# Windowed attention and a SiLU MLP: three bits of each weight's low word by ScalarE's output conversion, and one VectorE instruction less per weight tile

## The chip, the cores and the metric

The kernel runs on one core of a Trainium2 chip. The metric is the device time of one execution in microseconds. Three executions of the kernel before took 979.6, 981.55 and 981.93 us; the median is 981.55 us.

## What is computed

```python
def _attn_ref(q, k, v):                       # q, k, v: (8, 8, 576, 64)
    scores = scale * np.matmul(q, k.transpose(0, 1, 3, 2))
    rel = pos[:, None] - pos[None, :]
    bias = slopes[:, None, None] * (-np.abs(rel).astype(np.float32))[None, :, :]
    mask = (rel >= 0) & (rel < 128)
    scores = np.where(mask, scores + bias[None], -1000000000.0)
    attn = np.exp(scores - np.max(scores, axis=-1, keepdims=True))
    attn = attn / (np.sum(attn, axis=-1, keepdims=True) + 1e-09)
    return np.matmul(attn, v).astype(np.float32)

x = attn_out.transpose(0, 2, 1, 3).reshape(4608, 512)
h = x @ w_in                                  # w_in: (512, 2048)
out = ((h / (1 + np.exp(-h))) @ w_out).astype(np.float32)   # w_out: (2048, 512)
```

q, k and v are float32. The two weight matrices are float64: each value arrives as two 32-bit words.

## The kernel before, in words

The 4,608 tokens are 36 tiles of 128; four tiles are one group of 512, so there are nine groups. Attention runs over pairs (a tile and half of its eight heads): `scores` (PE), `row_max` (VectorE, L311, adds the bias and takes the maximum out of PSUM), `exps` (ScalarE, L321), a split of the result in a high and a low 16-bit part (`p_hi` on ScalarE, L330, and `p_lo` on VectorE, L335), a transpose by DMA (`hl<-hr`), and `attend` (PE, `av`, L381). The MLP runs over 16 slices `f` of 128 hidden columns: `gemm1` makes `h` in two halves, `act1` to `act4` make `gt` and its high and low parts `gh` and `gl` (ScalarE L498 and L511, VectorE L503, GpSimd L118), `gemm2` adds to the outputs `o`, also in two halves.

Products of float32 accuracy are made from a high and a low part of each operand, so each weight tile is needed as two tiles. There are 32 weight tiles of 128 x 512 values, 16 of each matrix. A weight tile is loaded as 128 x 1024 words (`wr`, by `w_load`) and converted in five steps:

- `w_split1`, ScalarE, L581: reads the high words (every second word) as float32 and scales them into `wm`, so that sign and exponent come to stand where a float32 wants them after a shift;
- `w_shift`, VectorE, L587: shifts `wm` left by 3 bits, in place;
- `w_low`, VectorE, L592: shifts the low words (every second word of `wr`) right by 29 and joins the three bits to `wm` with an or;
- `w_hi`, ScalarE, L602: rounds `wm` to the high part `w`;
- `w_lo`, GpSimd, L118: subtracts the high part from `wm`, which gives the low part.

`wm` has two buffers (the pool's default, tag `io`), so a split waits for the subtraction of the weight tile two before it. The high and low parts of a tile take the place of its raw words.

The order on each engine is the order of the program. It walks through positions; a position is one half of a `gemm1` or `gemm2`. `put` and `later` enter steps in a plan by position, and `begin` issues those that are due. In the first group, whose slices come as `gemm1` half 0, half 1, `gemm2` half 0, half 1, `w_next` is called at each half 0: it issues the split of the next weight tile and enters the other steps at the positions given by `WD`, counted from the split (shift and join one later, high part two, low part three), and the load of the ninth tile ahead. Three tiles are begun before the first group. The scores of eight to ten pairs are spread over the first group by the table `CLOSE` and the function `at`; from this group on the scores and `av` share the two PSUM buffers of tag `a`, so that `attend` can begin only when VectorE has read the scores in front of it.

Of the kernel before, what the change touches and what calls it, by code (L numbers as in the profile page):

```python
# [8 lines left out]
F16 = mybir.dt.float16  # L9
BF16 = mybir.dt.bfloat16  # L10
I32 = mybir.dt.int32
AF = mybir.ActivationFunctionType
ALU = mybir.AluOpType
AX = mybir.AxisListType
# [31 lines left out]
SIGN_UP = -(2.0**32)  # L46


SLICE = 4


# [5 lines left out]
XD = GT  # L57
EARLY = ("w0_15", "w1_15", "w0_14", "w1_14", "w0_12", "w1_12", "w0_13")
AHEAD = 9
WD = (1, 1, 2, 3)  # L60

CLOSE = (1, 5, 8, 14, 20, 26, 32, 38)

# [1 line left out]
def at(p):  # L65

    if p < 2 * GT:
        return STEP * (p - 2 * GT) - 18
    if p < 4 * GT:
        return CLOSE[p - 2 * GT]  # L70
    return STEP * (p - 2 * GT) - LEAD
# [3 lines left out]
def tile_window_attention_then_silu_mlp(ctx, tc, qk, v, w_in, w_out, base8, out):  # L75
    nc = tc.nc
# [12 lines left out]
    wraw = {}  # L89
# [22 lines left out]
    def f32(ap):  # L112
        return ap.bitcast(F32)
# [41 lines left out]
    def vscale_reduce(b, i):  # L155
# [9 lines left out]
        else:  # L165
            junk = pool.tile([P, DM], F32, tag="gt", name=f"vj{b}_{i}") if b == 0 else t
            nc.scalar.activation(junk, t, AF.Abs, accum_out=m)

    wsc = {}

    def w_stat(which, f):

        if f == 0:
            vred["w", which] = {"m": pool.tile([P, NF], F32, tag=f"stat{which}", bufs=1, name=f"stat{which}")}
        junk = pool.tile([P, DM], BF16, tag="xs", bufs=2, name=f"wj{which}_{f}")
        nc.scalar.activation(
            junk, f32(w_parts(f, which)[0]), AF.Square, accum_out=vred["w", which]["m"][:, f : f + 1]
        )

    def vscale_finish(b, stage):  # L180
# [5 lines left out]
        elif stage == 1:  # L186
# [4 lines left out]
            nc.vector.tensor_reduce(c, ps[:1, :P], axis=AX.X, op=ALU.max)  # L191
            nc.vector.tensor_single_scalar(c.bitcast(I32), c.bitcast(I32), 0x7F800000, op=ALU.bitwise_and)
            if isinstance(b, tuple):
                ci = c.bitcast(I32)
                nc.vector.tensor_single_scalar(ci, ci, 1, op=ALU.logical_shift_right)
# [4 lines left out]
            inv = col[:1, 2:3]  # L200
            nc.vector.tensor_single_scalar(inv.bitcast(I32), c.bitcast(I32), -(14 << 23), op=ALU.add)
            nc.vector.tensor_scalar(c.bitcast(I32), c.bitcast(I32), -1, 268 << 23, op0=ALU.mult, op1=ALU.add)
        else:
# [113 lines left out]
    def exps(p, u):  # L317
        t, n = st[p]["t"][u], (2 - blocks(p).start) * P
        for h in range(2):
            x = t[:, h, 2 * P - n :]  # L320
            nc.scalar.activation(x, x, AF.Exp, bias=st[p]["mx"][:, 2 * u + h : 2 * u + h + 1], scale=-1.0)  # L321

    def split_of(p, u, what):
        n = 2 - blocks(p).start
        return what[:, : 4 * n * P].rearrange("p (a h c) -> p a h c", a=2, h=2)

    def p_hi(p, u):
        t, n = st[p]["t"][u], (2 - blocks(p).start) * P
        st[p]["hr", u] = hr = pool.tile([P, 8 * P], F16, tag="hr", bufs=2, name=f"hr{p}_{u}")
        nc.scalar.activation(split_of(p, u, hr)[:, 0], t[:, :, 2 * P - n :], AF.Copy, scale=PSCALE)  # L330

# [23 lines left out]
    def p_hi_first(p, u):  # L355
        n = 2 - blocks(p).start
        st[p]["hl"][u] = hl = pool.tile([P, 8, P], F16, tag="hl", bufs=4, name=f"hl{p}_{u}")
        hi = hl[:, : 2 * n].rearrange("p a c -> p (a c)")
        nc.scalar.activation(hi, st[p]["pt", u], AF.Copy, scale=PSCALE)

# [94 lines left out]
    def x_parts(i, part):  # L455
        t, first = xt[i & -2, "t"][:, i % 2], i % GT * P
        cols, scale = slice(first, first + P), vsc[i // NBLK][:, 1:2]
        if part == 0:
            nc.scalar.activation(xh[:, :, cols], t[:, :NCC], AF.Copy, scale=scale)
            return  # L460
# [106 lines left out]
    def w_load(f, which):  # L567
        t = pool.tile([P, 1024], I32, tag=f"w{which}_{f}", bufs=1, name=f"wr{f}_{which}")
        wraw[(f, which)] = t
        if which == 0:  # L570
            nc.sync.dma_start(
                t.rearrange("p (c f) -> p c f", c=NCC),
                w_in.bitcast(I32)[:, f * 2 * P : (f + 1) * 2 * P].rearrange("(c p) f -> p c f", p=P),
            )
        else:
            nc.sync.dma_start(t, w_out.bitcast(I32)[f * P : (f + 1) * P, :])

    def w_split1(f, which):
        t = wraw[(f, which)].rearrange("p (n w) -> p n w", w=2)
        m = pool.tile([P, DM], F32, tag="io", name=f"wm{f}_{which}")  # L580
        nc.scalar.activation(m, t[:, :, 1].bitcast(F32), AF.Prelu, scale=HI_SCALE, alpha=SIGN_UP)  # L581
        wraw[(f, which)] = (t, m)

    def w_shift(f, which):
        t, m = wraw[(f, which)]
        mi = m.bitcast(I32)
        nc.vector.tensor_single_scalar(mi, mi, 3, op=ALU.logical_shift_left)  # L587

    def w_low(f, which):
        t, m = wraw[(f, which)]  # L590
        mi = m.bitcast(I32)
        nc.vector.scalar_tensor_tensor(  # L592
            out=mi, in0=t[:, :, 0], scalar=29, in1=mi, op0=ALU.logical_shift_right, op1=ALU.bitwise_or
        )

    def w_parts(f, which):
        if which == 0:
            return [weight(kind, f).rearrange("p a b -> p (a b)") for kind in ("wih", "wil")]
        return weight("woh", f), weight("wol", f)
# [54 lines left out]
    def put(point, fn, *a):  # L654
        plan.setdefault(max(point, at(0)), []).append((fn, a))

    for p in range(NPAIR):
        i, q = divmod(p, 2)
        n = at(p)
        if p == 2 * GT - 1:  # L660
            a = n + 2 * STEP - 1
        elif p == 2 * GT:
            a = n + 10
        elif p == 2 * GT + 1:
            a = n + 12
        else:
            a = n + (2 * STEP + 2 if p < 2 * GT else 15 if p < 4 * GT else 13)
# [45 lines left out]
    for which, n in enumerate((CONV_IN, CONV_OUT)):  # L713
        for f in range(NF):
            for k, fn in enumerate((conv1, conv2, conv3)):
                put(n + SLICE * f + (k if which or f else 0), fn, which, f)
    for g in range(1, NG):
        put(at(2 * GT * g) + 10, x_unit, g)
        if g >= IN16:
            put(g * SLICE * NF - 2, mlp_scales, g)  # L720
    for b in range(1, NBB):

        n = at(2 * GT * (NBLK * b // GT)) + 2
# [8 lines left out]
    def later(n, fn, *a):  # L732
        put(pos[0] + n, fn, *a)
# [9 lines left out]
    def w_next():  # L743
        if wi[1] < len(wq):
            a = wq[wi[1]]
            wi[1] += 1
            w_split1(*a)
            for fn, n in zip((w_shift, w_low, w_hi, w_lo), WD):
                later(n, fn, *a)
            later(1, w_next_load)  # L750

# [4 lines left out]
    with tc.manual_schedule():  # L756
# [25 lines left out]
        for n in (-19, -7, -2):  # L782
            put(n, w_next)
# [7 lines left out]
        for g in range(NG):  # L791
# [3 lines left out]
            for f in range(NF):  # L795
                n = g * NF + f
# [3 lines left out]
            n = g * NF + NF - 1  # L800
            seq += [("g2", n - 1, 0), ("g2", n - 1, 1), ("g2", n, 0), ("g2", n, 1)]
            for k, n, half in seq:
                if k == "xt":
                    x_transpose(half)
                    continue
                begin()
                x_send()
                if k == "g1":
                    gemm1(n, half)
                    if half == 1:  # L810
                        act1(n)
                        if n % NF == NF - 1:
                            turn_over(n)
                        else:
                            later(1, act2, n)
                            later(2, act3, n)
                            later(2, act4, n)
                else:
                    gemm2(n, half)
                    if n % NF == NF - 1:  # L820
                        store(g, 2 * half)
                        store(g, 2 * half + 1)
                if g == 0 and half == 0:
                    w_next()
                pos[0] += 1
# [38 lines left out]
```

## Time and profile before

| | |
|---|---|
| median of three runs | 981.55 us |
| the profiled execution | 982.2 us |
| its span | 980.4 us |
| mean granted TensorE clock | 0.984 |
| busy: PE, VectorE, ScalarE, GpSimd | 942.7, 622.6, 481.2, 142.7 us |
| first and last start of a weight's split (L581) | 39.7 and 172.1 us |
| its chain that ended last: PE, VectorE, ScalarE | 81%, 10%, 3% |

In the profile, PE is TensorE's matmuls, PEld its weight loads, DVE VectorE, ACT ScalarE, POOL GpSimd and SP the engine that issues the transfers. A row of a group gives line, engine and operation, the tiles written and read with their shapes, the count, then the busy time, the mean length of one in ns, and the idle time of the engine ahead of it with what ended that. A row of a timeline begins with start and length in us from the start of the span. A chain is followed back from the last instruction, at each step to what released it.

### The profile page before, as it was taken

Reading aid. Unit: us, or ns where it says so; the run is one execution under the profiler, and the core shown is the slowest. Engines: PE = TensorE matmul, PEld = TensorE weight load, DVE = VectorE, ACT = ScalarE, POOL = GpSimd, SP = SyncE. Lnnn points to the kernel's source line nnn. Section 1 sums busy time; section 2 is a strip of 40 time slices with the busy share of each in tenths; the row PEclk is TensorE's granted clock in tenths of the full one; section 3 lists DMA queues with packets and bytes.
Section 4 is the critical chain, followed back from the end, with each engine's and each line's share of the span. In section 5 each row is a group of like instructions: output and inputs, shape, how many; then the busy total and the mean of one; then the engine's idle time right before and its main releaser. Section 6 shows DMA issues by size and latency. Waiting matters only on the chain.

```text
span 980.4 us, 17282 instructions
## 1 busy us (share of the span) xinstructions
PE 942.7 (96%) x6572; PEld 581.6 (59%) x6572; DVE 622.6 (64%) x1567; ACT 481.2 (49%) x984; POOL 142.7 (15%) x129
## 2 busy tenths in 40 slices
PE   7978988999998999999999999999999999999998
PEld 6856766777776887654545554554555545554443
DVE  4888999655676887876666665555655565553222
ACT  5665665667553554555444445444544454433222
POOL 3154555222211222100000000000000000000000
PEclk8998999999998999999999999999999999999999
DMA  7848982423334543432364535332434343321001
GB/s 248 300 118 217 242 215 49 119 65 86 78 69 124 119 119 79 116 87 66 88 149 119 119 97 130 87 87 65 130 86 88 86 129 87 65 55 54 1 1 43
DMA packets 201075, 104.95 MB, mean 107 GB/s; under 512 B 168224, under 2 KB 176416, under 8 KB 200992
## 3 DMA queue, kind: packets, MB, share of 16 engines
q1 hardware_dynamic: 200992, 103.84, 41.4%
q8 instruction: 52, 0.85, 0.4%
q14 instruction: 31, 0.25, 0.1%
HBM read 54.00 MB, written 9.44 MB: 65 GB/s over the span
## 4 chain that ended last, share of the span: by engine, by line
PE 81%; DVE 10%; ACT 3%; DMA 2%; issue 2%; SPq 0%; POOL 0%; ACTq 0%; DVEq 0%; POOLq 0%
PE o L551 32%; PE h L485 30%; PE sp L291 7%; PE h L490 6%; PE av L381 5%; DVE wm L587 2%; DVE wm L592 2%; DMA early<-v 1%; DVE v L273 1%; DVE t L311 1%; DVE hr L335 1%; DVE gt L503 1%; ACT wm L581 1%; DMA hl<-hr 1%; ACT gt L498 1%
## 5 line engine op out<-in xcount | busy, mean ns | idle before, releaser
L551 PE MATMUL o<-w,gh 128*128 128x512 f16 (+1 forms) x1152 | 354.2, 389 | 0.0
L485 PE MATMUL h<-xt,w 128*128 128x512 f16 (+1 forms) x1536 | 317.8, 354 | 0.0
L498 ACT ACTIVATE gt<-h,gsc 128x512 f32<-128x512 f32 x112 | 77.1, 688 | 319.2 <-PE h L485 317.2
L551 PE MATMUL o<-w,gl 128*128 128x512 f16 (+1 forms) x576 | 222.8, 387 | 1.2 <-POOL gl L118 1.2
L485 PEld LDWEIGHTS <-w 128*128 128x128 f16 x1536 | 143.7, 98 | 130.8 <-issue 2.4
L503 DVE SCALAR_TENSOR_TENSOR gt<-gt,h 128x512 f32<-128x512 f32 x144 | 98.7, 686 | 176.6 <-ACT gt L498 176.3
L551 PEld LDWEIGHTS <-gh 128*128 128x128 f16 x768 | 74.9, 98 | 88.6
L321 ACT ACTIVATE t<-t,mx 128x256 f32<-128x256 f32 (+1 forms) x288 | 121.5, 486 | 12.0 <-DVE mx L311 11.9
L311 DVE CUSTOM_DVE_ANT_0 t<-sp,tab 128x256 f32<-128x256 f32 (+1 forms) x288 | 102.3, 403 | 18.6 <-PE sp L291 11.9
L519 DVE SCALAR_TENSOR_TENSOR gl<-gt,gh 128x512 f16<-128x512 f32 x96 | 66.5, 693 | 74.8 <-ACT gh L513 74.7
L335 DVE SCALAR_TENSOR_TENSOR hr<-t,hr 128x512 f16<-128x512 f32 (+1 forms) x128 | 99.2, 793 | 23.3 <-ACT hr L330 23.3
L490 PE MATMUL h<-xh,w 128*128 128x512 f32 x256 | 92.6, 416 | 4.6 <-ACT xh L434 3.6
L262 POOL TENSOR_SCALAR v<-rv,vsc 128x512 f16<-128x512 f32 x32 | 25.1, 785 | 444.4 <-DMA rv<-v 335.2
L118 POOL TENSOR_TENSOR gl<-gt,gh 128x512 fp32r<-128x512 f32 x45 | 63.2, 1405 | 177.5 <-ACT gh L511 141.5
L291 PEld LDWEIGHTS sp<-k,q 64*128 64x128 f32 x1088 | 69.5, 192 | 32.1 <-issue 31.1
L291 PE MATMUL sp<-k,q 64*128 64x128 f32 x1088 | 83.9, 291 | 4.7 <-DVE xs L408 4.6
L513 ACT ACTIVATE gh<-gt 128x512 f16<-128x512 f32 x96 | 60.0, 624 | 47.5 <-DVE gt L503 47.2
L551 PEld LDWEIGHTS o<-w,gh 128*128 128x128 f32 x384 | 71.9, 193 | 16.3 <-ACT gh L511 0.3
L381 PE MATMUL av<-v,hl 128*128 128x65 f16 (+1 forms) x1632 | 63.1, 194 | 15.3 <-DVE mx L311 8.4
L330 ACT ACTIVATE hr<-t 128x512 f16<-128x512 f32 (+1 forms) x128 | 75.9, 598 | 3.6 <-DMA hl<-hr 3.6
L381 PEld LDWEIGHTS <-hl 128*128 128x128 f16 x1632 | 58.5, 98 | 31.8 <-issue 19.0
L551 PEld LDWEIGHTS <-gl 128*128 128x128 f16 x384 | 37.5, 98 | 47.8 <-DVE gl L519 3.5
(99 smaller groups left out, 789.2 us busy)
## 6 DMA issues: line engine op xcount, KB each, us to landing
q<-qk SPq DMA_DIRECT2D x36, 256.0 KB, 3.0
k<-qk SPq DMA_DIRECT2D x36, 256.0 KB, 3.1
out<-ot SPq DMA_DIRECT2D x36, 256.0 KB, 2.4
wr<-w_in SPq DMA_DIRECT2D x16, 512.0 KB, 6.8
wr<-w_out SPq DMA_DIRECT2D x16, 512.0 KB, 6.0
rv<-v SPq DMA_DIRECT2D x32, 256.0 KB, 2.9
vm<-v SPq DMA_DIRECT2D x27, 256.0 KB, 3.3
early<-v SPq DMA_DIRECT2D x9, 256.0 KB, 5.2
```

Of the source, the lines that this page charges most:

```text
L291: nc.tensor.matmul(sp[h][:, u, o], qs[i][rows, 2 * q + u], ks[i - 1 + o][rows, 2 * q + u], start=True, stop=True, skip_group_check=True,)
L311: nc.vector.tensor_tensor_reduce(out=t[:, h, 2 * P - n :], in0=st[p]["sp"][h][:, u, o].rearrange("p o c -> p (o c)"), in1=tab[:, 4 * q + 2 ...
L321: nc.scalar.activation(x, x, AF.Exp, bias=st[p]["mx"][:, 2 * u + h : 2 * u + h + 1], scale=-1.0)
L330: nc.scalar.activation(split_of(p, u, hr)[:, 0], t[:, :, 2 * P - n :], AF.Copy, scale=PSCALE)
L335: nc.vector.scalar_tensor_tensor(out=hr[:, 1], in0=t[:, :, 2 * P - n :], scalar=PSCALE, in1=hr[:, 0], op0=ALU.mult, op1=ALU.subtract)
L381: nc.tensor.matmul(av[:, 2 * u + h, : rhs.shape[-1]], lhs, rhs, start=(n == 0), stop=(n == len(seq) - 1), skip_group_check=True,)
L485: nc.tensor.matmul(o, w[:, wp, cc], x, start=start and k == 0, stop=stop, skip_group_check=True)
L490: nc.tensor.matmul(hps[n], w[:, cc], x, start=(half == 0 and i == 0), stop=(half == 1 and i == len(seq) - 1), skip_group_check=True,)
L498: nc.scalar.activation(gt, hps[n], AF.Tanh, scale=scale)
L503: nc.vector.scalar_tensor_tensor(out=gt, in0=gt, scalar=1.0, in1=hps[n], op0=ALU.add, op1=ALU.mult)
L519: nc.vector.scalar_tensor_tensor(out=gl, in0=gt, scalar=CUT, in1=gh, op0=ALU.mult, op1=ALU.subtract)
L551: nc.tensor.matmul(ops[ti], a[:, t], w, start=(f == 0 and i == 0), stop=(f == NF - 1 and i == len(seq) - 1), skip_group_check=True,)
```

## The change

ScalarE gets a second conversion for each weight tile, directly behind the split: it reads the low words as unsigned integers, scales them by nearly 2^-29 and adds a bias, so that the conversion of its output to an integer leaves the top three bits as a number from 0 to 7; this is written back in place of the low word. VectorE's two instructions become one, which shifts `wm` left by 3 and joins the number with an or. The separate shift is gone, and `WD` has one entry less; the other steps keep their positions.

```diff
+LOW3 = 2.0**-29 * (1 - 2.0**-10)
+LOW3_UP = 7.5 * 2.0**-10 - 0.5
...
-WD = (1, 1, 2, 3)
+WD = (1, 2, 3)
...
-    def w_shift(f, which):
-        t, m = wraw[(f, which)]
-        mi = m.bitcast(I32)
-        nc.vector.tensor_single_scalar(mi, mi, 3, op=ALU.logical_shift_left)
-
-    def w_low(f, which):
+    def w_low3(f, which):
+
+        t, _ = wraw[(f, which)]
+        low = t[:, :, 0]
+        nc.scalar.activation(low, low.bitcast(U32), AF.Copy, scale=LOW3, bias=LOW3_UP)
+
+    def w_join(f, which):
         t, m = wraw[(f, which)]
         mi = m.bitcast(I32)
         nc.vector.scalar_tensor_tensor(
-            out=mi, in0=t[:, :, 0], scalar=29, in1=mi, op0=ALU.logical_shift_right, op1=ALU.bitwise_or
+            out=mi, in0=mi, scalar=3, in1=t[:, :, 0], op0=ALU.logical_shift_left, op1=ALU.bitwise_or
         )
...
             w_split1(*a)
-            for fn, n in zip((w_shift, w_low, w_hi, w_lo), WD):
+            w_low3(*a)
+            for fn, n in zip((w_join, w_hi, w_lo), WD):
                 later(n, fn, *a)
```

The order of the instructions changes on VectorE and ScalarE alone. One place in the first group, first VectorE's queue of the kernel before, from the join of one weight tile (`wm_0_1447`) to the first row maximum of the second half of a pair (`t_1_1515`); ISA is the row maximum and its read-out:

```order
L592 SCALAR_TENSOR_TENSOR wm_0_1447<-wr_0_1006,wm_0_1447 128x512
L120 SCALAR_TENSOR_TENSOR x_1469<-xs_1449,x_1469 128x256
L311 ISA t_0_1494,mx_1482<-sp_0_1472,tab 128x256
L311 ISA mx_1482 128x1
L311 ISA t_0_1494,mx_1482<-sp_1_1473,tab 128x256
L311 ISA mx_1482 128x1
L164 TENSOR_REDUCE vmx_884<-vm_5_1415 128x1
L587 TENSOR_SCALAR wm_1_1492<-wm_1_1492 128x512
L592 SCALAR_TENSOR_TENSOR wm_1_1492<-wr_1_1063,wm_1_1492 128x512
L311 ISA t_1_1515,mx_1482<-sp_0_1472,tab 128x256
```

And the same place after the change (its lines are four or five further down; L597 is the new join):

```order
L597 SCALAR_TENSOR_TENSOR wm_0_1447<-wm_0_1447,wr_0_1006 128x512
L124 SCALAR_TENSOR_TENSOR x_1469<-xs_1450,x_1469 128x256
L315 ISA t_0_1495,mx_1482<-sp_0_1472,tab 128x256
L315 ISA mx_1482 128x1
L315 ISA t_0_1495,mx_1482<-sp_1_1473,tab 128x256
L315 ISA mx_1482 128x1
L168 TENSOR_REDUCE vmx_884<-vm_5_1416 128x1
L597 SCALAR_TENSOR_TENSOR wm_1_1492<-wm_1_1492,wr_1_1063 128x512
L315 ISA t_1_1515,mx_1482<-sp_0_1472,tab 128x256
```

One instruction in front of the row maxima is gone, and nothing else has moved. ScalarE's queue at this place before, from the high part of that weight tile to the exponentials (L321) of the pair's second half:

```order
L602 CAST w_8_1483<-wm_0_1447 128x512
L581 ACTIVATE wm_1_1492<-wr_1_1063 128x512
L498 ACTIVATE gt_1513<-h_1485 128x512
L321 ACTIVATE t_0_1494<-t_0_1494,mx_1482 128x256 x2
L602 CAST w_7_1522<-wm_1_1492 128x512
L581 ACTIVATE wm_0_1531<-wr_0_1122 128x512
L321 ACTIVATE t_1_1515<-t_1_1515,mx_1482 128x256 x2
```

And after the change (L592 is now the new conversion on ScalarE):

```order
L607 CAST w_8_1483<-wm_0_1447 128x512
L585 ACTIVATE wm_1_1492<-wr_1_1063 128x512
L592 ACTIVATE wr_1_1063<-wr_1_1063 128x512
L502 ACTIVATE gt_1513<-h_1485 128x512
L325 ACTIVATE t_0_1495<-t_0_1495,mx_1482 128x256 x2
L607 CAST w_7_1522<-wm_1_1492 128x512
L585 ACTIVATE wm_0_1531<-wr_0_1122 128x512
L592 ACTIVATE wr_0_1122<-wr_0_1122 128x512
L325 ACTIVATE t_1_1515<-t_1_1515,mx_1482 128x256 x2
```

Behind each split there is one more instruction, ahead of the hidden activation and of the exponentials. The transfers, GpSimd's and PE's queues are as before.

More of the change, by code (lines that the diff above doesn't have):

```diff
@@ L11 @@
 I32 = mybir.dt.int32
+U32 = mybir.dt.uint32
 AF = mybir.ActivationFunctionType
```

## Prediction

> **What bounds the kernel now.** I read the head of the page first, then the windows by stage, because a share of the whole span mixes stages.
>
> ```profile
> span 980.4 us, 17282 instructions
> PE 942.7 (96%) x6572; PEld 581.6 (59%) x6572; DVE 622.6 (64%) x1567; ACT 481.2 (49%) x984; POOL 142.7 (15%) x129
> ```
>
> PE is busy for 96% of the span, so only the places where PE is idle or slow can give anything back. The weights are converted while the first group of tokens is multiplied. The tile of the converted word, `wm`, tells when that is:
>
> ```profile
> L581 ACT ACTIVATE wm<-wr x32: 657/668/692, 39.7 to 172.1; 128x512 f32<-128x512 f32 x32
> L587 DVE TENSOR_SCALAR wm<-wm x32: 404/981/1521, 40.4 to 172.8; 128x512 int32<-128x512 int32 x32
> L592 DVE SCALAR_TENSOR_TENSOR wm<-wr,wm x32: 691/693/1679, 40.8 to 173.8; 128x512 int32<-128x512 int32 x32
> ```
>
> All of it starts between 39.7 and 173.8 us. The windows (length, then busy us of PE, PEld, DVE, ACT and POOL, then the granted clock, the DMA share and GB/s) of the two halves of this stage and of three short stretches:
>
> ```profile
> 62.00:134.60 72.60, 63.85 (x417) 49.61 (x416) 66.69 (x137) 46.35 (x92) 39.10 (x28) 0.93 0.89 222
> 134.60:178.00 43.40, 40.00 (x264) 31.57 (x264) 39.09 (x74) 25.52 (x50) 26.10 (x20) 1.00 0.42 109
> 76.90:80.30 3.40, 3.40 (x10) 2.63 (x10) 2.96 (x7) 1.24 (x3) 0.00 (x0) 0.56 1.49 239
> 90.50:93.90 3.40, 3.40 (x30) 2.82 (x27) 3.33 (x7) 3.40 (x9) 2.14 (x2) 0.57 0.78 292
> 128.10:131.50 3.40, 3.40 (x30) 2.83 (x28) 2.62 (x7) 1.96 (x5) 1.28 (x1) 0.56 1.21 223
> ```
>
> While weights are converted, VectorE is busy 66.69 of 72.60 us (92%) and then 39.09 of 43.40 (90%). ScalarE is busy only 64% and 59%. PE is idle 8.75 + 3.40 = 12.15 us, and in three stretches of 3.4 us its clock is 0.56, so each costs it about 1.5 us more. Who keeps PE waiting, in the list of waits of 40 to 184 us (total, times, longest):
>
> ```profile
> PE av L381 <- DVE mx L311: 8.4, 7, 2.4
> PE h L490 <- ACT xh L434: 3.6, 1, 3.6
> PE av L381 <- DMA q<-qk: 2.2, 1, 2.2
> PE sp L291 <- DVE xs L408: 1.1, 1, 1.1
> ```
>
> The attention products `av` wait for VectorE's row maxima (L311), which release the PSUM buffer that `av` takes. Those instructions are late because VectorE reaches them late. The chain that ended last, cut to 36 to 178 us, says what made it late:
>
> ```profile
> by line: DVE wm L587 14.9%; DVE wm L592 13.6%; PE h L490 10.1%; issue 9.8%; DVE hr L335 7.0%; ACT wm L581 5.4%; DMA hl<-hr 4.7%; DVE v L273 3.6%; DVE t L311 3.4%; DVE gt L503 3.1%; PE o L551 2.9%; DMA vm<-v 2.1%; DVE vmx L164 2.0%; PE av L3
> ```
>
> Of these 142 us the shift (L587) holds 21.2 and the join (L592) 19.3. So a microsecond saved there is, to begin with, a microsecond of the program.
>
> **The change: what VectorE is spared.** 32 shifts go; they take 27.1 us in all, by the row of the group:
>
> ```profile
> L587 DVE TENSOR_SCALAR wm<-wm 128x512 int32<-128x512 int32 x32 | 27.1, 848 | 5.5 <-ACT wm L581 5.2
> ```
>
> But a shift alone takes 0.40 us (its shortest, above) against a mean of 0.85; the rest is waiting inside the instruction. The next rows show for what, and the place that I re-lay by hand. It is the timeline of 106 to 118 us, first VectorE's, then ScalarE's and GpSimd's (start, length):
>
> ```profile
> 109.12 1.52 DVE L587 TENSOR_SCALAR wm<-wm 128x512 int32<-128x512 int32 x1
> 110.67 0.69 DVE L592 SCALAR_TENSOR_TENSOR wm<-wr,wm 128x512 int32<-128x512 int32 x1
> ...
> 112.90 0.83 DVE L587 TENSOR_SCALAR wm<-wm 128x512 int32<-128x512 int32 x1
> 113.77 0.69 DVE L592 SCALAR_TENSOR_TENSOR wm<-wr,wm 128x512 int32<-128x512 int32 x1
> ...
> 115.80 1.02 DVE L587 TENSOR_SCALAR wm<-wm 128x512 int32<-128x512 int32 x1
> 116.85 0.69 DVE L592 SCALAR_TENSOR_TENSOR wm<-wr,wm 128x512 int32<-128x512 int32 x1
> ...
> 111.45 0.62 ACT L602 CAST w<-wm 128x512 fp32r<-128x512 f32 x1 [2.79 <-DVE wm L592]
> 111.98 0.67 ACT L581 ACTIVATE wm<-wr 128x512 f32<-128x512 f32 x1
> 112.55 0.58 ACT L498 ACTIVATE gt<-h 128x512 f32<-128x512 f32 x1
> 113.03 0.89 ACT L321 ACTIVATE t<-t,mx 128x256 f32<-128x256 f32 x2
> 114.55 0.62 ACT L602 CAST w<-wm 128x512 fp32r<-128x512 f32 x1 [0.62 <-DVE wm L592]
> ...
> 108.60 1.75 POOL L118 TENSOR_TENSOR gl<-gt,gh 128x512 fp32r<-128x512 f32 x1
> 112.15 1.30 POOL L118 TENSOR_TENSOR w<-wm,w 128x512 fp32r<-128x512 f32 x1 [1.80 <-ACT w L602]
> 115.24 1.28 POOL L118 TENSOR_TENSOR w<-wm,w 128x512 fp32r<-128x512 f32 x1 [1.80 <-ACT w L602]
> ```
>
> GpSimd's subtraction ends at 110.35, 113.45 and 116.52, and each long shift ends 0.3 us behind that: it got to work 0.1 us before GpSimd was done. So shift and join can be held by a GpSimd instruction (the join's longest is 1.68 us). The join usually escaped (median 0.693) because the shift ahead of it had sat out the wait. By the medians the join would cost 0.69 and VectorE would be spared all 27.1 us. [...] So I count 32 x 0.40 = 12.9 us of VectorE time as gone and the 14.2 us of waiting as mostly inherited.
>
> **What ScalarE gets.** 32 more conversions. No row shows this one (unsigned integer in, integer out, every second word written). The nearest row is L581, which reads every second word of the same tile and takes 0.67; below it lies L602 with 0.62 (above), and as the upper end I allow two passes, 1.34. I take 0.67. In ScalarE's queue it costs 0.57, the distance from L581 to L498 (111.98 to 112.55). That is 18 us more in a stage in which it is idle for over a third; but ScalarE works in order, so the exponentials, `gt` and `gh` behind each split come 0.57 later than the split lets them, and the join has to wait for the second conversion.
>
> **Re-laid by hand**, with the first join ready at 109.12: it is held till 110.24, ends at 110.93 and not at 111.36 (0.43 gained). ScalarE's L602 follows at 111.02, L581 at 111.55, the new conversion from 112.12 to 112.79; GpSimd has the port till about 112.90. VectorE is ready at 112.47, so the second join runs from 112.90 to 113.59 instead of ending at 114.46: 0.87 gained, and the `av` that waits for the two row maxima behind it comes 0.87 earlier. For the third weight ScalarE is the one behind: L498 and the exponentials end at about 114.06, so L602 starts at 113.97 (0.58 earlier), the new conversion ends at 115.74, GpSimd's port is free at 115.85, the join ends at 116.54, not 117.54. The exponentials behind it start at 115.64 instead of 115.66, so what waits for them on VectorE gains only about 0.6. Three weights thus give between 0.6 and 1.0: 0.2 to 0.33 each, and 0.43 where nothing behind it is late. Where VectorE waits for the split anyway, the loop of one weight is this:
>
> ```profile
> 137.74 0.67 ACT L581 ACTIVATE wm<-wr 128x512 f32<-128x512 f32 x1
> ...
> 138.44 1.05 DVE L587 TENSOR_SCALAR wm<-wm 128x512 int32<-128x512 int32 x1 [0.29 <-ACT wm L581]
> 139.53 0.69 DVE L592 SCALAR_TENSOR_TENSOR wm<-wr,wm 128x512 int32<-128x512 int32 x1
> ...
> 137.91 1.29 POOL L118 TENSOR_TENSOR w<-wm,w 128x512 fp32r<-128x512 f32 x1 [1.33 <-ACT w L602]
> ```
>
> Now it ends at 140.22. After the change the conversion ends at 137.74 + 0.57 + 0.67 = 138.98, GpSimd at 139.20, and the join at 139.89: 0.33 gained.
>
> **The sum.** 21.2 us of shifts on the path at 0.85 are 25 weights; at 0.3 each that is 7.5 us (0.2 gives 5.0; 0.43 gives 10.8). The three slow-clock stretches follow the longest waits of PE, 2.2 to 2.4 us; waits of about 1.1 us are followed by none there. With 0.9 off, some go: 3 x 1.5 us, of which I take half, since VectorE still bounds the stage: 2.2 (0 to 4.5). At the start PE waits 3.6 us for ScalarE's `xh` (L434), which has two splits in front of it; there the conversion comes on top, less the shift's wait between them: 0.6 lost (0 to 1.2). 7.5 + 2.2 - 0.6 = 9.1; the ends are 3.8 and 15.3. The stages behind contain no weight conversion and stay. The profiled execution took 982.2 us, 1.8 around its span, and 0.65 over the median of 981.55; so 973.1 on its own scale and **972.5** against the median.
>
> **Rivals.**
>
> *More: PE is fed.* If VectorE's spared time also breaks up the meetings with GpSimd (joins pass before GpSimd starts), PE's 12.15 us of idle time and the 4.5 us of slow clock go almost whole: 14 to 16.6, about 966. For it: with all 27 us gone, VectorE's 105.8 busy us of these 116 (91%) would be about 79 (68%). Against it: GpSimd's subtraction follows L602, and the join follows the next split, so they keep meeting.
>
> *Nothing: the path goes over ScalarE.* In the hand-laid piece the third weight was already ScalarE's. If the exponentials, `hr` and `gh` are late by 0.57 in most rounds, or the `hl` transfers (4.7% of the chain, under a DMA share of 0.89) decide, the 7.5 shrink to under 3 and the slow stretches stay: about 980.
>
> *Less: the strided write is dearer.* No ScalarE row writes every second word. If the new conversion takes 1.0 us, midway between 0.67 and 1.34, the loop at 137 us gains nothing (138.98 becomes 139.31, and the join ends at 140.0 to 140.2), the second weight of the hand-laid piece gains 0.6 and the third about 0.3. At 0.2 for the 25 weights and no slow stretch less, 5 - 0.6 = 4.4 are left: about 977.5. L581's strided read, 0.05 over L602, speaks against it. [...]
>
> *Slower: the new conversion takes two passes.* It turns the sign from about 1.1 us on. At 1.34, the loop loses 0.34 for each of the 12 splits on the chain (5.4% of 142 us at 0.67), 4 us; the exponentials behind the others come over 1 us late, which eats what their joins gain: about 986. For it speaks only that no row converts to an integer on ScalarE; against it, that L581 and L602 differ in function, type and stride and lie within 0.05.
>
> That the join is not what it says (two inputs swapped, a shift in front of an or) I price at nothing: the same form already runs in 0.69 with its strided input.
>
> **Chances.** The forecast 0.65, more 0.12, nothing 0.12, less 0.04, slower 0.07. About 0.3% (3 us) is what a measurement of this kernel can tell from no change. The forecast's lower end, 3.8, is still outside that, and so is "less": faster 0.81, same 0.12, slower 0.07. The range takes in the forecast's two ends and a little of both neighbours: 966 to 979.
>
> **What would show it.** Right: `wm` has one VectorE row with a mean well over 0.69 (0.9 to 1.1, waits inherited), the new ScalarE row at 0.62 to 0.72, VectorE still busy for 85 to 90% of the stage, the waits of `av` for L311 at about half of 8.4 us, one or two slow-clock stretches fewer, and everything behind the first group shifted and otherwise alike. Wrong: a ScalarE row over 1 us; waits of VectorE for `hr` (L335) or `gt` that grow by what the shift gave; or a join at 0.69 in the mean, which would mean that the wait for GpSimd went with the shift.

## The result, and the profile after

The changed kernel's median is 971.95 us over four runs (970.19 to 974.15), beside 980.85 us for the kernel before; the ratio on record is 0.9901, with a 95% interval of 0.9872 to 0.993 (the two medians alone give 0.9909). Measured once more later, beside other kernels, it gave 971.93 us and 0.9904 (0.988 to 0.9928). It is faster by about 9 us; the prediction was 972.5 us, faster by 9.1. One run of the kernel before among the later ones, 1197.39 us at a granted clock of 0.75, is left out of every comparison.

The head of the page after:

```profile
span 971.5 us, 17272 instructions
PE 938.7 (97%) x6572; PEld 578.0 (59%) x6572; DVE 597.0 (61%) x1535; ACT 497.3 (51%) x1016; POOL 141.6 (15%) x129
```

VectorE has lost 25.6 us of busy time and ScalarE gained 16.1, and the span is 8.9 us shorter. The conversion of the weights, by the instructions on `wm` (L597 is the new join, L607 the high part) and by those on the raw words `wr` (L592 is the new conversion):

```profile
L585 ACT ACTIVATE wm<-wr x32: 649/665/689, 40.5 to 163.3; 128x512 f32<-128x512 f32 x32
L597 DVE SCALAR_TENSOR_TENSOR wm<-wm,wr x32: 679/716/1777, 41.7 to 164.6; 128x512 int32<-128x512 int32 x32
L607 ACT CAST w<-wm x32: 603/618/624, 42.5 to 165.4; 128x512 fp32r<-128x512 f32 x32
```

```profile
L592 ACT ACTIVATE wr<-wr x32: 647/658/672, 41.0 to 163.9; 128x512 int32<-128x512 uint32 x32
```

The first split starts 0.8 us later than before (40.5, was 39.7), the last 8.8 us earlier (163.3, was 172.1). The 0.8 us are no cost of the change: they stand ahead of the first new instruction, and the first splits of the fourteen profiles lie between 39.3 and 41.0 us. The groups add the idle time ahead of the join, which the shift and the old join had as 5.5 and 1.1 us. First the old join before, then the new join after:

```profile
L592 DVE SCALAR_TENSOR_TENSOR wm<-wr,wm 128x512 int32<-128x512 int32 x32 | 27.0, 845 | 1.1
```

```profile
L597 DVE SCALAR_TENSOR_TENSOR wm<-wm,wr 128x512 int32<-128x512 int32 x32 | 29.4, 918 | 15.0 <-issue 8.0 <-ACT wr L592 7.0
```

The scores, one instruction group per pair, show where on the way the time was won. Their starts before (start, length), at five places of the first group and the next:

```profile
62.10 1.16 PE L291 MATMUL sp<-k,q 64*128 64x128 f32 x16
...
82.55 1.16 PE L291 MATMUL sp<-k,q 64*128 64x128 f32 x16
...
134.59 1.16 PE L291 MATMUL sp<-k,q 64*128 64x128 f32 x16
...
172.29 1.16 PE L291 MATMUL sp<-k,q 64*128 64x128 f32 x16
...
189.23 0.72 PE L291 MATMUL sp<-k,q 64*128 64x128 f32 x8
```

and after:

```profile
62.60 1.16 PE L295 MATMUL sp<-k,q 64*128 64x128 f32 x16
...
78.74 1.34 PE L295 MATMUL sp<-k,q 64*128 64x128 f32 x16
...
129.13 1.16 PE L295 MATMUL sp<-k,q 64*128 64x128 f32 x16
...
163.83 1.16 PE L295 MATMUL sp<-k,q 64*128 64x128 f32 x16
...
179.21 0.72 PE L295 MATMUL sp<-k,q 64*128 64x128 f32 x8
```

0.5 us behind at 62 us, 3.8 ahead two pairs later, 5.5 at 134, 8.5 at 172, 10.0 at 189; from there to the start of the last product (976.19 us before, 966.43 after) the distance stays within 0.3, and behind it 0.9 us are lost on the way to the spans' 8.9. Of the 10.0, 8.5 are won while weights are converted; up to 3 of these are two slow-clock stretches fewer between 62 and 178 us, three before and one after, at an estimated 1.5 us each (3.4 us at a clock of 0.56 to 0.58). The last 1.5 come behind the last split: the profile before has a slow-clock stretch there, which the profile after lacks:

```profile
182.70:186.10 3.40, 3.35 (x26) 2.87 (x26) 1.80 (x3) 1.47 (x3) 0.00 (x0) 0.56 0.62 45
```

The windows of the stage after the change, with the one slow-clock stretch that is left between 62 and 178 us, and PE's waits:

```profile
62.00:134.60 72.60, 66.93 (x454) 51.60 (x454) 58.30 (x133) 58.74 (x116) 41.56 (x30) 0.98 0.97 238
134.60:178.00 43.40, 40.94 (x278) 32.36 (x278) 32.37 (x74) 33.52 (x65) 22.45 (x17) 1.00 0.35 89
121.90:125.30 3.40, 2.72 (x28) 2.46 (x29) 1.90 (x9) 3.06 (x6) 1.28 (x1) 0.58 0.98 213
```

```profile
PE av L385 <- DVE mx L315: 5.5, 5, 2.4
PE h L494 <- ACT xh L438: 3.2, 1, 3.2
PE av L385 <- DVE v L277: 1.7, 2, 1.2
```

PE's idle time in the first window fell from 8.75 to 5.67 us, its clock rose from 0.93 to 0.98, and VectorE is busy 80% instead of 92%. In the chain, cut to 36 to 170 us, VectorE's work on `wm` held 28.5% before:

```profile
by line: PE h L494 15.7%; PE o L555 10.4%; DMA vm<-v 10.0%; issue 8.5%; DMA hl<-hr 5.2%; DVE wm L597 4.9%; DMA wr<-w_out 4.6%; PE sp L295 4.4%; ACT wr L592 3.2%; DVE v L277 3.0%; ACT t L325 3.0%; ACT wm L585 2.9%; PE av L385 2.6%; ACT hr L3
```

Now the join has 4.9% of it, the new conversion 3.2%. PE's products lead, and the transfers `vm<-v`, `hl<-hr` and `wr<-w_out` hold 19.8% together.

### The profile page after: what moved, and what is told of

Its sections match the earlier page's. It is cut to its first block, busy times and chain, and to the rows that moved or that the text cites. A ratio compares the mean times of both kernels' runs of the same rounds, so it can differ in the third digit from the quotient of the medians.

```text
span 971.5 us, 17272 instructions
## 1 busy us (share of the span) xinstructions
PE 938.7 (97%) x6572; PEld 578.0 (59%) x6572; DVE 597.0 (61%) x1535; ACT 497.3 (51%) x1016; POOL 141.6 (15%) x129
## 4 chain that ended last, share of the span: by engine, by line
PE 84%; DVE 5%; DMA 4%; ACT 4%; issue 2%; SPq 1%; POOL 0%; ACTq 0%; DVEq 0%; POOLq 0%
PE o L555 33%; PE h L489 30%; PE sp L295 7%; PE h L494 7%; PE av L385 5%; DMA vm<-v 1%; DMA early<-v 1%; DVE v L277 1%; DVE t L315 1%; DMA hl<-hr 1%; DVE gt L507 1%; DVE wm L597 1%; DMA wr<-w_out 1%; ACT gt L502 1%; PE pt L357 1%
## 5 line engine op out<-in xcount | busy, mean ns | idle before, releaser
L339 DVE SCALAR_TENSOR_TENSOR hr<-t,hr 128x512 f16<-128x512 f32 (+1 forms) x128 | 93.4, 747 | 24.4 <-ACT hr L334 24.4
L122 POOL TENSOR_TENSOR gl<-gt,gh 128x512 fp32r<-128x512 f32 x45 | 60.1, 1336 | 185.2 <-ACT gh L515 142.8
L555 PEld LDWEIGHTS o<-w,gh 128*128 128x128 f32 x384 | 69.9, 188 | 16.5 <-ACT gh L515 1.2
```

Source lines behind the costliest of these rows:

```text
L339: nc.vector.scalar_tensor_tensor(out=hr[:, 1], in0=t[:, :, 2 * P - n :], scalar=PSCALE, in1=hr[:, 0], op0=ALU.mult, op1=ALU.subtract)
L555: nc.tensor.matmul(ops[ti], a[:, t], w, start=(f == 0 and i == 0), stop=(f == NF - 1 and i == len(seq) - 1), skip_group_check=True,)
```

## The experiments

The theory: VectorE's queue sets the time of the stage; the bare instruction is gone, the wait for GpSimd is inherited, the conversion is nearly hidden. The rivals: ScalarE carries the path now, or VectorE's waits are slack. Ratios are to the kernel before, on the same chip, with 95% intervals. For each kernel the row of its VectorE instructions on `wm` is shown: busy time, mean, and the idle time ahead of them. The ratio of the changed kernel itself is known to about 0.002 (0.9901 and 0.9904), so a distance of 2 us or less from it is not told apart from none.

**1. The conversion added, the shift kept.** Against the kernel after:

```diff
-WD = (1, 2, 3)
+WD = (1, 1, 2, 3)
...
+    def w_shift(f, which):
+        _, m = wraw[(f, which)]
+        mi = m.bitcast(I32)
+        nc.vector.tensor_single_scalar(mi, mi, 3, op=ALU.logical_shift_left)
...
-            out=mi, in0=mi, scalar=3, in1=t[:, :, 0], op0=ALU.logical_shift_left, op1=ALU.bitwise_or
+            out=mi, in0=t[:, :, 0], scalar=0, in1=mi, op0=ALU.logical_shift_right, op1=ALU.bitwise_or
...
-            for fn, n in zip((w_join, w_hi, w_lo), WD):
+            for fn, n in zip((w_shift, w_join, w_hi, w_lo), WD):
```

> The ScalarE conversion of after, but the separate shift is kept, so VectorE has two instructions per weight tile as before. Theory (VectorE's queue sets the time, the conversion is nearly hidden): the shift starts at the end of the split as before and lasts longer than the conversion, so only what stands behind the split on ScalarE is later: 981 to 984 us, 0 to 3 over before. Rival (ScalarE carries a good part of the path, and the conversion goes through to the end): 0.57 us at 12 to 25 of the weights, 987 to 994.

983.33 us, ratio 1.0021 (1.0012 to 1.003): with the shift kept, the conversion costs about 2 us, within the 0 to 3 of the theory.

```profile
L597 DVE TENSOR_SCALAR wm<-wm 128x512 int32<-128x512 int32 x32 | 28.7, 897 | 4.8 <-ACT wm L585 4.7
L602 DVE SCALAR_TENSOR_TENSOR wm<-wr,wm 128x512 int32<-128x512 int32 x32 | 23.1, 721 | 3.1
```

**2. The join without the conversion.** The low words go into the join unconverted:

```diff
-            out=mi, in0=mi, scalar=3, in1=t[:, :, 0], op0=ALU.logical_shift_left, op1=ALU.bitwise_or
+            out=mi, in0=mi, scalar=3, in1=t[:, :, 0], op0=ALU.logical_shift_left, op1=ALU.bitwise_and
...
-            w_low3(*a)
```

> After without the ScalarE conversion: the join shifts the high word and ands it with the unconverted low word, so the weights' low bits are wrong; one VectorE instruction with two inputs as in after, ScalarE as in before. Theory: the join is held by GpSimd about as long as by the conversion (139.20 against 138.98 in the loop worked out for 137 us), so little comes back: 969 to 972. Rival (the conversion on ScalarE is what keeps the gain at 9 us): 960 to 966.

971.87 us, ratio 0.9901 (0.9888 to 0.9915): taking the conversion out of the changed kernel gives nothing, as the theory had it.

```profile
L597 DVE SCALAR_TENSOR_TENSOR wm<-wm,wr 128x512 int32<-128x512 int32 x32 | 36.9, 1154 | 6.3 <-ACT wm L585 6.2
```

The row says why. The idle time ahead of the join fell from 15.0 to 6.3 us, and the join itself grew from 29.4 to 36.9: ready earlier, it waits inside for GpSimd (its median is 1.20 us, 0.72 after the change). The sums, 44.4 and 43.2 us, are nearly the same. What such a wait looks like, the profile after shows: the five joins that meet no GpSimd instruction take 0.68 to 0.69 us, and the longest, 1.78 us, starts 0.12 us behind one and ends 0.55 us behind its end:

```profile
144.28 1.35 POOL L122 TENSOR_TENSOR gl<-gt,gh 128x512 fp32r<-128x512 f32 x1 [0.35 <-POOL w L122]
...
144.40 1.78 DVE L597 SCALAR_TENSOR_TENSOR wm<-wm,wr 128x512 int32<-128x512 int32 x1
```

**3. The conversion twice as long.** A ScalarE instruction of 448 columns between split and conversion (0.596 us, its median):

```diff
+    junk = const.tile([P, 448], BF16, name="junk")
...
+        nc.scalar.activation(junk, t[:, :448, 1].bitcast(F32), AF.Copy, scale=HI_SCALE)
         nc.scalar.activation(low, low.bitcast(U32), AF.Copy, scale=LOW3, bias=LOW3_UP)
```

> After with one more ScalarE instruction of about 0.6 us between the split and the conversion (it writes 448 columns that nobody reads), so that the join waits as if the conversion took 1.3 us. By the prediction's price for a conversion of 1.34 us: about 986, all of the gain lost and more. Rival (ScalarE's spare time still hides it, since VectorE comes late to most joins): 973 to 978.

978.42 us, ratio 0.9971 (0.996 to 0.9981). The prediction's price for such a conversion, 986, was 8 us too high, and the rival's range, 973 to 978, is missed by 0.4. It is 6.5 us over the changed kernel: behind GpSimd's subtraction there is room for one conversion, not for two. Of the 32 joins 15 wait for the conversion, 16.2 us in all; after the change 11 did, 7.0 us.

```profile
L599 DVE SCALAR_TENSOR_TENSOR wm<-wm,wr 128x512 int32<-128x512 int32 x32 | 25.2, 787 | 25.7 <-ACT wr L594 16.2 <-POOL w L123 6.4 <-issue 3.0
```

**4. The join as a one-input reduction.**

```diff
-        mi = m.bitcast(I32)
-        nc.vector.scalar_tensor_tensor(
-            out=mi, in0=mi, scalar=3, in1=t[:, :, 0], op0=ALU.logical_shift_left, op1=ALU.bitwise_or
-        )
+        nc.vector.tensor_reduce(m[:, 0:1], t[:, :, 0].bitcast(F32), axis=AX.X, op=ALU.max)
```

> After with the join replaced by a VectorE reduction over the converted low words, which has one input and the same 512 columns (the weights are not joined, so their values are wrong); every wait and the order stay. It cannot be held by GpSimd: 0.68 us each instead of a mean of 0.92. Theory (the inherited wait for GpSimd is the part of the shift's time that did not come back): 7.6 us less on VectorE, about half of it at the end, 966 to 970. Rival (those waits are slack): 971 to 973.

969.48 us, ratio 0.988 (0.9863 to 0.9897): about 2.4 us under the changed kernel, at the upper end of the theory's range and hardly clear of the noise. The instruction is never stretched (0.665 to 0.696 us, 0.683 in the mean), but the idle time ahead of it stays:

```profile
L596 DVE TENSOR_REDUCE wm<-wr 128x1 f32<-128x512 f32 x32 | 21.8, 683 | 15.0 <-issue 8.0 <-ACT wr L592 6.9
```

**5. Both taken away.** As 4, without the conversion, and with a minimum of integers as the reduction:

```diff
...
+        nc.vector.tensor_reduce(m[:, 0:1].bitcast(I32), t[:, :, 0], axis=AX.X, op=ALU.min)
...
-            w_low3(*a)
```

> Both taken away at once: no ScalarE conversion, and the join replaced by a one-input VectorE reduction of the same 512 columns over the raw low words, which GpSimd cannot hold (weights not joined, values wrong). Taken away alone, the conversion gave 0 and the two-input join 2.4 us against after. Theory (conversion and GpSimd's subtraction run side by side between two joins, each hides the other): 963 to 967, clearly more than the sum. Rival (the two are independent): 968.5 to 970.5.

964.49 us, ratio 0.9818 (0.9805 to 0.983). Alone, the two gave 0 and 2.4 us; together they give 7.5, which is well outside the noise. So the conversion and GpSimd's subtraction run side by side and each hides the other.

```profile
L596 DVE TENSOR_REDUCE wm<-wr 128x1 int32<-128x512 int32 x32 | 21.7, 680 | 5.8 <-ACT wm L585 5.6
```

**6. The conversion a tile ahead.**

```diff
-        t, _ = wraw[(f, which)]
-        low = t[:, :, 0]
+        low = wraw[(f, which)].rearrange("p (n w) -> p n w", w=2)[:, :, 0]
...
+            if wi[1] == 1:
+                w_low3(*a)
             w_split1(*a)
-            w_low3(*a)
+            if wi[1] < len(wq):
+                w_low3(*wq[wi[1]])
```

> After with the ScalarE conversion of each weight tile issued behind the split of the tile before it, so that the join finds it done and waits for the split alone; same instructions, same result. Theory (the join is held by GpSimd's subtraction until about where the conversion ends, so the conversion's place does not matter): 970.5 to 973.5, no difference from after. Rival (the joins' 7.0 us of waiting for the conversion is lost time): 966 to 969.

973.35 us, ratio 0.9913 (0.9892 to 0.9934): no gain, the theory's case. The join no longer waits for the conversion, and is stretched by GpSimd for it:

```profile
L596 DVE SCALAR_TENSOR_TENSOR wm<-wm,wr 128x512 int32<-128x512 int32 x32 | 37.7, 1179 | 7.5 <-ACT wm L585 7.5
```

**7. The shift alone.** The kernel before without `w_low`:

```diff
-WD = (1, 1, 2, 3)
+WD = (1, 2, 3)
...
-            for fn, n in zip((w_shift, w_low, w_hi, w_lo), WD):
+            for fn, n in zip((w_shift, w_hi, w_lo), WD):
```

> The kernel before without the second VectorE instruction and without any ScalarE conversion: the three low bits are left out of each weight, the shift (0.40 us alone) remains. Against after it has 0.3 us less VectorE work per weight tile and the same meetings with GpSimd. Theory (bare VectorE time on the path goes through at about 0.7, waits are inherited): 32 x 0.3 x 0.7 = 6.7 less than after, but PE's own time is near, so 965 to 969. Rival (the wait for GpSimd is now all that counts, however short the instruction): 970 to 973.

965.96 us, ratio 0.9846 (0.9827 to 0.9866), 6 us under the changed kernel and in the theory's range. The shift keeps its waits (mean 0.883, against 0.848 in the kernel before). Kernel 2 has no conversion either and a join in the shift's place, of 0.671 us at its shortest where the shift has 0.405; it is 5.9 us slower, so the shorter bare instruction comes through.

```profile
L587 DVE TENSOR_SCALAR wm<-wm 128x512 int32<-128x512 int32 x32 | 28.3, 883 | 7.2 <-ACT wm L581 7.1
```

**8. Nine reductions moved from VectorE to ScalarE.**

```diff
-        if b > 0 or i % 2:
+        if b > 1 or b == 0 and i % 2:
```

> After with the nine reductions that look for the largest absolute value of the second pair of batches (VectorE, 0.68 us each, all in the stage of the weight conversion) given to ScalarE, as sums of absolute values as for the first pair; the result keeps its accuracy. Theory (VectorE's queue still sets the time of the stage, ScalarE has room): 6.1 us less on VectorE at about 0.7 gives 967 to 969. Rival (ScalarE is as near to the path as VectorE, as the longer conversion showed with 6.5 us for 18 us more): 971 to 974.

973.33 us, ratio 0.9919 (0.9903 to 0.9936). The theory in its simple form, that any microsecond off VectorE counts, falls here.

```profile
L597 DVE SCALAR_TENSOR_TENSOR wm<-wm,wr 128x512 int32<-128x512 int32 x32 | 29.4, 918 | 21.5 <-issue 15.1 <-ACT wr L592 5.2 <-POOL gl L122 1.2
```

**9. The same without the conversion** (edits of 2 and 8).

> The nine reductions for the largest absolute value on ScalarE, and no ScalarE conversion (low words anded in unconverted, values wrong), so ScalarE has less work than in after and VectorE 6.1 us less. Theory (with the conversion in place ScalarE was as near to the path as VectorE, which is why moving the reductions gave nothing): 966 to 969. Rival (VectorE's single-input work is no longer on the path at all): 971 to 973.

972.22 us, ratio 0.9899 (0.9883 to 0.9915). So it was not ScalarE's fullness alone that swallowed the gain of 8.

```profile
L597 DVE SCALAR_TENSOR_TENSOR wm<-wm,wr 128x512 int32<-128x512 int32 x32 | 39.4, 1230 | 9.3 <-ACT wm L585 9.1
```

In 8, the idle time ahead of the join is 6.5 us longer than after; in 9, idle and busy time are 5.5 us longer than in 2. So the 6.1 us of reductions had filled time in which VectorE would otherwise wait for the next join. In the profile of 8, PE's waits for the row maxima did fall, from 5.5 to 1.6 us; what took that gain is not shown.

**10. High and low part a position later.**

```diff
-WD = (1, 2, 3)
+WD = (1, 3, 4)
```

> After with the high part and the low part of each weight tile one position later, so that ScalarE does the next tile's split and conversion first and GpSimd's subtraction starts only after the next join has begun; same instructions, same result. Theory (a join that does not meet GpSimd takes 0.69 and waits for the conversion alone): the mean of the join falls below 0.8 and 2 to 4 us are gained, 968 to 970. Rival (the meetings move to VectorE's other two-input instructions, such as the one that writes hr): 971 to 974.

989.77 us, ratio 1.0081 (1.0069 to 1.0094). Half of the theory came true, the join's mean is 0.747; the time went the other way. ScalarE's waits tell why:

```profile
L597 DVE SCALAR_TENSOR_TENSOR wm<-wm,wr 128x512 int32<-128x512 int32 x32 | 23.9, 747 | 37.2 <-ACT wr L592 22.4 <-issue 13.5 <-POOL v L266 1.4
```

```profile
ACT wm L585 <- POOL w L122: 38.0, 24, 2.7
```

The split needs one of the two `wm` buffers, and GpSimd, which now has `gl` ahead of the subtraction in its queue, gives it back late.

**11. High and low part together.** `WD = (1, 3, 3)`.

> After with the high part one position later as in the kernel that measured 989.8 us, but the low part entered at the same position as the high part, so that GpSimd's queue has the subtraction ahead of the gl that is due there and the two wm buffers come free earlier; same instructions, same result. Theory (the joins are spared the meeting, and it was the late release of wm that cost 18 us): ScalarE's wait for wm falls from 35 us to under 10 and the time to 967 to 971. Rival (two buffers are too few for this order whatever GpSimd's queue): 975 to 990.

972.97 us, ratio 0.9904 (0.9883 to 0.9924): 17 us of the loss are back, so GpSimd's queue was most of it. But nothing is won over the changed kernel, the expected 967 to 971 are missed, and ScalarE's wait for `wm` is 11.6 us where under 10 was expected.

```profile
L597 DVE SCALAR_TENSOR_TENSOR wm<-wm,wr 128x512 int32<-128x512 int32 x32 | 26.8, 837 | 13.9 <-ACT wr L592 7.7 <-issue 3.4 <-POOL gl L122 2.5
```

```profile
ACT wm L585 <- POOL w L122: 11.6, 18, 1.1
```

**12. The changed kernel again.**

> The changed kernel once more, beside the others on one chip, for the size of the gain and for its profile in another execution: 970 to 974 us, 8 to 10 below before, the join's mean between 0.85 and 1.0 us.

971.93 us; its join has a mean of 0.917 us. No kernel that carries the three bits into the weights beat it; kernel 7, which leaves them out, is 6 us faster.

Put side by side, by the time that VectorE spends on the weights' joins, inside and ahead of them:

| kernel | busy + idle ahead, us | ratio |
|---|---|---|
| 5, reduction, no conversion | 21.7 + 5.8 = 27.5 | 0.9818 |
| 7, shift alone | 28.3 + 7.2 = 35.5 | 0.9846 |
| 4, reduction | 21.8 + 15.0 = 36.8 | 0.9880 |
| 2, no conversion | 36.9 + 6.3 = 43.2 | 0.9901 |
| after | 29.4 + 15.0 = 44.4 | 0.9901 |
| 6, conversion ahead | 37.7 + 7.5 = 45.2 | 0.9913 |
| 3, conversion twice as long | 25.2 + 25.7 = 50.9 | 0.9971 |
| 1, conversion and shift | 28.7 + 4.8 + 23.1 + 3.1 = 59.7 | 1.0021 |
| before | 27.1 + 5.5 + 27.0 + 1.1 = 60.7 | 1 |

From 60.7 to 27.5 us the time falls by 0.0182, or 17.9 us: a bit over half a microsecond for each. It does so on average only: a straight line through the nine has 0.6 us for each and misses single kernels by up to 1.7 us. These nine differ in the steps of the weight conversion alone. Kernels 8 and 9 lie 3 to 4 us under that line and 10 lies 6 over it; 11 lies within 1.3.

## Why the prediction was right, point by point

**Where the time is** was right: in the profiled pair the stage with the weight conversion gives 8.5 of the 10.0 us, and a slow-clock stretch that is missing behind it gives the other 1.5.

**The bare shift is gone, the wait is inherited** was right, and it is the point on which the size hung. That the join would inherit the wait was the author's reading of three shifts that end 0.3 us behind a GpSimd instruction. What the prediction's hand-laid piece calls GpSimd's port is the end of such an instruction less 0.1 us (110.24 for 110.35); a port as such no run shows. The join's mean is 0.918 us (forecast 0.9 to 1.1), its longest 1.78. By the table, VectorE's time on the joins fell by 16.3 us where the prediction counted 12.9, so of the 14.2 us of waiting about 10.8 were inherited. Part of them is now a wait for the conversion. Kernel 5, whose reduction is never stretched (0.665 to 0.689 us) and waits for no conversion, shows what lay in the two together: 7.5 us more.

**The conversion**, taken at 0.67 us, takes 0.659; two passes or a dear strided write are refuted. That it is hidden is shown by kernel 2, and by what it is shown by kernels 5 and 6. The hand-laid loop of one weight can be laid beside rows of the profile after, ScalarE's, GpSimd's and VectorE's:

```profile
109.16 0.60 ACT L607 CAST w<-wm 128x512 fp32r<-128x512 f32 x1
109.67 0.69 ACT L585 ACTIVATE wm<-wr 128x512 f32<-128x512 f32 x1
110.26 0.66 ACT L592 ACTIVATE wr<-wr 128x512 int32<-128x512 uint32 x1
...
109.84 1.30 POOL L122 TENSOR_TENSOR w<-wm,w 128x512 fp32r<-128x512 f32 x1 [2.07 <-ACT w L607]
...
111.02 0.69 DVE L597 SCALAR_TENSOR_TENSOR wm<-wm,wr 128x512 int32<-128x512 int32 x1 [0.63 <-ACT wr L592]
```

From the split's start to the join's end there are 2.04 us; the prediction had 2.15 (137.74 to 139.89), the kernel before 2.48. Conversion and subtraction end within 0.25 us of each other (110.92 and 111.14), as worked out. The loop gained 0.44 there, not 0.33, because the join got to work 0.1 us before GpSimd was done; the prediction had read this off the long shifts and left it out of its loop.

**The sum** came out at 9.1, measured 8.9. As far as the noise lets one say, its terms were off by one to one and a half microseconds and cancel, which is luck.

The 50 runs of the kernel before that were taken beside the experiments average 981.5 us at a mean clock of 0.987, the ten runs of the changed kernel 972.1 at 0.989: 9.4 apart. At a mean clock of 0.99 or more, 13 and 5 of them are 9.8 apart (980.1 and 970.3); from 0.987 to 0.989, 12 and 4 are 7.5 apart. A straight line of time against clock through all 60, with one step between the kernels, puts the step at 8.3. That leaves an estimated 1.1 us to the slow-clock term, where the sum had 2.2; by the two classes alone it could be anything from nothing to 1.9. The difference of the clocks, 0.0024, is an estimated 1.6 stretches, as one of them (1.5 of 980 us) lowers the mean by 0.0015; one or two fewer were forecast.

The 8.3 us are path and start together, where the sum had 7.5 - 0.6 = 6.9. The loss of 0.6 at the start came out as a small gain: PE waits 3.2 us for `xh`, not over 3.6. The conversion does cost 0.6 there, as kernel 2 without it waits 2.6, but the shifts that are gone save more.

**VectorE busy for 85 to 90%** was wrong: 80%. Part of the wait moved out of the instruction and stands ahead of it as idle time, 15.0 us, where the shift and the old join had 6.6. **The waits of `av`** for the row maxima were to halve; they fell from 8.4 to 5.5 (4.5 in the second profile).

**The rivals.** "More" fell: joins and subtractions do meet. "Nothing, the path goes over ScalarE" fell with the 9 us themselves. But ScalarE is as near as GpSimd: kernel 2, where taking the conversion away gave nothing, and kernel 5, where it did count, show that the two hide each other. "Less" and "slower" fell with the conversion's 0.659 us; the price of "slower" was wrong as well, 978.4 instead of 986 for 1.3 us, since only 15 of the 32 joins waited for the longer conversion.

**What the prediction had too simple** is its first step, that a microsecond saved on VectorE is one of the program. By the table it holds to about half for the ring of high part, split, conversion beside subtraction, and join. By kernels 8 and 9 it does not hold for one-input work between the joins, which fills waiting time. Why the ring passes on about half of what it is spared, and which of its waits would come next, stays open; a third `wm` buffer, which would tell in kernels 10 and 11, was not tried.

## What to carry to other kernels

When an instruction's mean is well above its shortest, count only the shortest as gone with it, and look for who inherits the wait; here about three quarters of the waiting was inherited. Work may be put on another engine for nothing where it runs beside something that the next step waits for anyway, and up to that length only: here one conversion of 0.66 us cost nothing behind a subtraction of 1.3, two cost 6.5 us. And judge a VectorE saving by the ring it lies in: 16.3 us fewer on the ring gave 9, 6.1 us fewer beside it gave none.

## What the hardware showed that was not expected

Where two instructions run side by side in front of a third, taking one of them away changed little here: 0 and 2.4 us, against 7.5 for both. A wait for GpSimd shows inside VectorE's join, as a mean of 1.15 us in kernel 2, where the shortest takes 0.67, and not as idle time, so that the busy shares of VectorE here overstate its work. A ScalarE instruction that reads and writes every second word, and converts from an unsigned to a signed integer, takes 0.659 us for 512 columns, no more than the split's 0.666, which only reads that way.
